# Halving the second batch as well, with smaller loads for the halves and new numbers in the planner's table

## The chip, the cores and the metric

The kernel runs on one core of one Trainium2 chip. The metric is the device time of one execution in microseconds. The kernel before took 1117.67 us, the median of three runs (1117.41 to 1120.12). The profiled execution, from which every duration below is taken, took 1118.3 us, and the span from its first to its last instruction is 1116.5 us.

## What is computed

Two layers, one after the other. The first is attention over 8 batches of 8 heads, 576 positions and 64 numbers per head, in which only scores within `tau` of the row's maximum count. The second is a feed-forward network that mixes each position with the one before it.

```python
# attention, for each batch and head
scores = q @ k.T / 8
thresh = scores.max(-1) - tau
attn = softmax(where(scores >= thresh, scores, -1e9))
x[:, :, head] = attn @ v                      # x: (8, 576, 512)
# feed-forward, on all heads together
x_prev = x shifted by one position
xk = mu_k * x + (1 - mu_k) * x_prev
xr = mu_r * x + (1 - mu_r) * x_prev
k = maximum(xk @ w_k, 0)                      # 512 -> 1024
out = sigmoid(xr @ w_r) * (k * k @ w_v)       # 1024 -> 512
```

## The kernel before

**Attention.** The heads go in four pairs. A *job* is one pair of one batch: `operands` loads `raw` (L408: 128 rows, 64 for each head, with 576 columns of queries, 64 of the last keys and 576 of keys, 1216 columns in all), scales the queries (ACT, L412), rounds everything to `hi` (ACT, L430) and takes the rest `lo` = raw - hi on POOL in two instructions, one for the queries and one for the keys (L436). Eight DMAs within the core's own memory (L455) then stack `hi` and `lo` above each other in `st1` and `st2` for each head, so that a matmul sees both. The first two jobs skip this splitting. `raw` has two buffers, `hi` and `lo` one, `st1` and `st2` three each, of which a job needs two.

A job is worked off in *units*: four units P of 128 queries, each for both heads, and one unit T with the last 64 queries of both heads. A unit counts 2 (P) or 1 (T) on the planner's scale of keys, a whole job 9. For each unit PE makes scores (L517, L506 or L492) in a bank `s`, of which there are two for each half of a unit; DVE takes the maximum (L551), ACT the exponential (L567), DVE masks and sums (L575), POOL normalizes (L600), PE transposes (L624) into one of four banks `w`, and ACT or DVE copies that to `pm` and `pl` (L642, L644). When a group of 256 queries is there, `attend` multiplies it with `v` (L704; two P units, with the T unit's 64 queries in one of the two groups), and DVE copies the result to `xT` and `xE` (L644).

**Feed-forward.** `ffn_chunk` handles 256 positions: POOL and DVE mix (L797, L806), ACT and POOL split (L819, L827), PE multiplies with `w_k` (L849), `w_r` (L891) and `w_v` (L913), DVE makes the product (L919), and the result is stored (L929). There are 18 chunks, two for each batch and two for the last 64 positions of four batches each. A chunk needs a group of 256 queries of all four pairs. The weights come as 20 pieces, each loaded (L338) and brought to two parts by ACT, four DVE instructions (L355, L369, L376, L386), ACT and POOL (L393, L397), with parts of `xT` of the odd batches as scratch.

**Halves.** In batch 0 the four pairs are gone through twice: first with units 0 and 1, then with units 2, T and 3. So the first chunk has its positions after four half jobs. Each half is a job of its own and loads and splits all 1216 columns again, though it uses only its own queries. Batches 1 to 7 are not halved: four jobs of T, 0, 1, 2, 3, after which both their chunks are ready.

**Order.** Nothing is scheduled at run time. Every step is put into a `Plan` with an engine, an assumed duration (`occ`), a key and the buffers it uses; `Plan.order` simulates the engines with these numbers and places, again and again, the step that can start first, with the smaller key at equal times. What it gives is the order of instructions on each engine. PE, ACT, DVE and POOL then run theirs in order, and all loads, shifts and stores stand in one queue, SP's. Feed-forward steps on PE have keys above those of attention (which have 1000 taken off), and so fill PE where attention isn't ready. `LATE` adds 0.3 us to the moment at which attention's steps on PE count as ready, from the planner's time `FROM` on, so that a feed-forward step is put in front where one is there.

Of the kernel before, what the change touches and what calls it, by code (L numbers as in the profile page):

```python
# [8 lines left out]
F32 = mybir.dt.float32  # L9
FR = mybir.dt.float32r  # L10
# [38 lines left out]
class Plan:  # L49
# [3 lines left out]
    HOP, LATE, FROM = 0.05, 0.3, 150.0  # L53
# [58 lines left out]
    def order(self, loose=()):  # L112
# [23 lines left out]
        pipe = 0.0  # L136
# [78 lines left out]
def tile_threshold_attention_then_rwkv_ffn(  # L215
    ctx: ExitStack,
    tc: tile.TileContext,
    qk: bass.AP,
    v: bass.AP,
# [8 lines left out]
    V, A, G, PE, SY = nc.vector, nc.scalar, nc.gpsimd, nc.tensor, nc.sync  # L228

    P = 128
# [10 lines left out]
    KT = S  # L243
    W = 2 * S + ST
# [78 lines left out]
    def weight(j, name, w, c, f, key, wait):  # L323
# [8 lines left out]
        def t():  # L332
# [21 lines left out]
            0.46,  # L354
# [8 lines left out]
        def word(y):  # L363
# [4 lines left out]
            0.46,  # L368
# [6 lines left out]
            0.7,  # L375
# [9 lines left out]
            0.7,  # L385
# [18 lines left out]

    def operands(job, key):
        b, hp = job["b"], job["hp"]
        raw = job["raw"] = sbuf("raw", [P, W], F32, 2)
        add("DMA", DQ, lambda: SY.dma_start(raw.get(), qk[b, hp]), writes=[raw], key=key - PREP - 5, kb=576)  # L408
        add(
            "ACT",  # L410
            0.67,
            lambda: A.activation(raw.get()[:, 0:S], raw.get()[:, 0:S], AF.Copy, scale=small.get()[:, 2:3]),  # L412
            reads=[(small, 2)],
            writes=[raw],
            key=key - PREP,
        )
# [12 lines left out]
        hi, lo = job["hi"], job["lo"] = sbuf("hi", [P, W], FR), sbuf("lo", [P, W], FR)  # L429
        add("ACT", 1.1, lambda: A.activation(hi.get(), raw.get(), AF.Copy), reads=[raw], writes=[hi], key=key - PREP)  # L430
        for y in range(2):
            cs = slice(0, S) if y == 0 else slice(S, W)
            add(
                "POOL",
                1.41 + 0.15 * y,
                lambda cs=cs: G.tensor_tensor(  # L436
                    lo.get()[:, cs], raw.get()[:, cs], hi.get()[:, cs].bitcast(F32), op=ALU.subtract
                ),
                reads=[raw, hi],
                writes=[(lo, y)],  # L440
                key=key - PREP,
            )
        job["st"] = [(sbuf("st1", [P, W], FR, 3), sbuf("st2", [P, S], FR, 3)) for _ in range(2)]
        for h in range(2):
            sl = slice(h * D, (h + 1) * D)
            t1, t2 = job["st"][h]

            up, dn = slice(0, D), slice(D, P)
            for dst, rows, src, n, r in (
                (t1, up, hi, W, (hi, None)),  # L450
                (t2, dn, hi, S, (hi, None)),
                (t1, dn, lo, W, (lo, None)),
                (t2, up, lo, S, (lo, 0)),
            ):
                fn = (lambda dst=dst, rows=rows, src=src, n=n, sl=sl: SY.dma_start(  # L455
                    dst.get()[rows, 0:n].bitcast(F32), src.get()[sl, 0:n].bitcast(F32)
                ))
                add("DMA", DQ, fn, reads=[r], writes=[(dst, rows.start)], key=key - PREP, kb=n // 4)

# [3 lines left out]
    def scores(unit, ss, key):  # L463
        job, c = unit["job"], unit["c"]
        raw = job["raw"]

        def keys(y, z):
            k0 = KT + (ST if unit["kind"] == "P" and y == 0 else 0)
            return slice(k0 + z * HS, k0 + (z + 1) * HS)

        if unit["kind"] == "T" and not job["plain"]:

            hi, lo = job["hi"], job["lo"]
            for v_, src in enumerate((raw, lo)):
                for h in range(2):
# [5 lines left out]
                            bd.get()[sl, v_, sl], src.get()[sl, SM:S].bitcast(F32), AF.Copy  # L481
# [14 lines left out]
        if unit["kind"] == "T" or job["plain"]:  # L496
# [3 lines left out]
            def both():  # L500
                for z in range(2):
                    for h in range(2):
                        hr = slice(h * D, (h + 1) * D)
                        o = ss[1].get()[hr, z, 0:HS] if last else ss[h].get()[:, z, 0:HS]
                        q = slice(SM, S) if last else slice(c * P, (c + 1) * P)
                        PE.matmul(o, raw.get()[hr, q], raw.get()[hr, keys(h, z)], start=True, stop=True)  # L506

            occ = 1.2 if last or key > COLD else 2.3
# [18 lines left out]
    def softmax(unit):  # L527
# [56 lines left out]
        def invert():  # L584
# [5 lines left out]
            0.29,  # L590
# [27 lines left out]
    def transposes(p, y, at, key, to):  # L618
# [9 lines left out]
        occ = 0.109 * len(at)  # L628
# [125 lines left out]
    def ffn_chunk(kind, b0, g, key):  # L754
# [35 lines left out]
        for hc in range(0, NCT, 2):  # L790
# [9 lines left out]
            for j in range(2):  # L800
# [14 lines left out]
                add("DVE", 0.8 if nseg == 1 else 1.57, scale, reads=[diff, mu_sb, *sr], writes=[d], key=key)  # L815
# [122 lines left out]
    halved = {0: ([0, 1], [2, "T", 3])}  # L938
# [3 lines left out]
    for b in range(B):  # L942
        for part, order in enumerate(halved.get(b, (["T", 0, 1, 2, 3],))):
            for hp in range(NPAIR):
                job = dict(ji=len(jobs), b=b, hp=hp, first=n, groups={}, plain=len(jobs) < PLAIN, units=[])
                job.update(tail="T" in order, tg=int(part == 1))
# [89 lines left out]
```

## Time and profile before

| | before |
|---|---|
| median of three runs | 1117.67 us |
| the profiled execution | 1118.3 us, span 1116.5 us |
| PE busy | 1037.2 us (93%) |
| DVE busy | 785.5 us (70%) |
| ACT busy | 736.0 us (66%) |
| POOL busy | 578.6 us (52%) |
| DMA traffic | 117.78 MB, mean 105 GB/s |

The chain of work that ended last runs on PE for 73% of the span, on DVE for 13%, on ACT for 6% and on DMA for 4%. Shares of the whole span hide that the kernel has three stages; the table of windows below shows them apart. In a window's row the figures are its length, then for each engine the busy time with the count of instructions, then the clock granted to PE, the share of the time that the DMA engines were busy, and GB/s. In rows of groups, the last parts are busy time and mean of one, and then the idle time ahead of the group with what ended it. In rows of waits they are the sum, the number of times and the longest one.

### The profile page before, as it was taken

The numbers are of one execution on the slowest core, as the hardware profiler recorded it, in microseconds if no ns is written. First come the engines' busy times: TensorE is split into PE (matmuls) and PEld (weight loads), VectorE is DVE, ScalarE is ACT, GpSimd is POOL, SyncE is SP. The second block draws the span as 40 slices with busy tenths as digits, with TensorE's granted clock in tenths as the row PEclk, the third lists the DMA queues.
The fourth block names the chain that finished last, engine by engine and source line by source line (L and its number), as shares of the span: only waits on it lengthen the run. The fifth ranks groups of instructions, "written<-read, shape, count | busy, mean of one in ns | idle before, by whom it ended". The sixth has DMA issues, their size and how long they took to land.

```text
span 1116.5 us, 19374 instructions
## 1 busy us (share of the span) xinstructions
PE 1037.2 (93%) x6832; PEld 852.4 (76%) x6832; DVE 785.5 (70%) x1712; ACT 736.0 (66%) x1543; POOL 578.6 (52%) x582
## 2 busy tenths in 40 slices
PE   5767878898999999999999999999999989999998
PEld 3446656776877878778789878886788869788887
DVE  6889988877878878877887749765888488422220
ACT  5676776675885876776878666775687557344443
POOL 3575765544564555554656535554465544444441
PEclk8777989999999999999999999999999999999999
DMA  6997365544444435444455314441544141000000
GB/s 218 241 269 226 92 162 132 127 113 119 103 102 119 118 84 139 116 110 111 111 130 137 89 43 121 101 108 37 128 115 118 34 92 39 19 20 20 20 19 19
DMA packets 40639, 117.78 MB, mean 105 GB/s; under 512 B 6752, under 2 KB 6752, under 8 KB 40544
## 3 DMA queue, kind: packets, MB, share of 16 engines
q1 hardware_dynamic: 40544, 116.55, 41.0%
q8 instruction: 55, 0.90, 0.3%
q14 instruction: 40, 0.33, 0.1%
HBM read 44.70 MB, written 9.44 MB: 48 GB/s over the span
## 4 chain that ended last, share of the span: by engine, by line
PE 73%; DVE 13%; ACT 6%; DMA 4%; issue 3%; POOL 1%; SPq 0%; POOLq 0%; ACTq 0%
PE w L913 16%; PE w L849 15%; PE w L704 11%; PE w L624 11%; PE s L517 10%; PE w L891 8%; DVE p L575 4%; PE s L492 2%; ACT p L567 2%; DVE sm L551 2%; DMA raw<-in_qk 1%; DVE sm L585 1%; DMA st<-lo 1%; DMA wk<-in_w_k 1%; DVE mk L806 1%
## 5 line engine op out<-in xcount | busy, mean ns | idle before, releaser
L600 POOL TENSOR_SCALAR p<-p,sm 128x576 f32<-128x576 f32 x288 | 225.5, 792 | 268.9 <-DVE sm L586 227.1
L575 DVE SCALAR_TENSOR_TENSOR p<-s,sm,p 128x576 f32<-128x576 f32 x288 | 232.4, 813 | 58.3 <-ACT p L567 57.1
L551 DVE TENSOR_REDUCE sm<-s 128x1 f32<-128x576 f32 x288 | 210.8, 751 | 40.6 <-PE s L517 27.9
L849 PE MATMUL w<-xk,wk 128*128 128x256 f32 x1728 | 231.0, 284 | 0.0
L913 PE MATMUL w<-wv,k 128*128 128x512 f32 x864 | 221.1, 397 | 0.0
L849 PEld LDWEIGHTS w<-xk,wk 128*128 128x128 f32 x1728 | 216.5, 190 | 1.2 <-issue 0.5
L624 PE MATMUL w<-ident,p 128*128 128x128 f32 x1312 | 197.0, 285 | 19.8 <-POOL p L600 14.8
L567 ACT ACTIVATE p<-s,sm 128x576 f32<-128x576 f32 x288 | 210.2, 730 | 0.6
L624 PEld LDWEIGHTS w<-ident,p 128*128 128x128 f32 x1312 | 156.5, 145 | 58.3 <-POOL p L600 32.1
L913 PEld LDWEIGHTS w<-wv,k 128*128 128x128 f32 x864 | 156.4, 189 | 28.7 <-issue 0.8
L642 ACT ACTIVATE pm<-w 128x512 f32<-128x512 f32 x169 | 99.7, 593 | 98.2 <-PE w L624 96.8
L704 PE MATMUL w<-pm,v 128*64 128x256 f32 (+1 forms) x1024 | 148.4, 425 | 5.2 <-DVE pm L644 4.3
L806 DVE SCALAR_TENSOR_TENSOR mk<-m,mu_sb,xT 128x256 f32<-128x256 f32 x128 | 88.6, 732 | 83.5 <-POOL xk L827 83.4
L517 PE MATMUL s<-st 128*128 128x288 f32 x496 | 119.1, 322 | 27.3 <-DVE p L575 11.7
L827 POOL TENSOR_TENSOR xk<-mk,xk 128x512 fp32r<-128x512 f32 x72 | 94.0, 1306 | 92.8 <-ACT xk L819 87.2
L559 ACT ACTIVATE sm<-sm,small 128x1 f32<-128x1 f32 x288 | 83.5, 290 | 83.4 <-DVE sm L551 80.3
L872 POOL TENSOR_TENSOR k<-r,k 128x512 fp32r<-128x512 f32 x72 | 93.8, 1304 | 81.8 <-ACT k L862 81.5
L704 PEld LDWEIGHTS w<-pm,v 128*64 128x64 f32 x1024 | 71.6, 141 | 64.1 <-issue 10.3
L517 PEld LDWEIGHTS s<-st 128*128 128x128 f32 x496 | 79.7, 193 | 51.4 <-issue 29.0
L436 POOL TENSOR_TENSOR lo<-raw,hi 128x576 fp32r<-128x576 f32 x68 | 102.1, 1518 | 31.2 <-ACT hi L430 23.7
L517 PE MATMUL s<-st,st 128*128 128x288 f32 x496 | 110.6, 305 | 0.0
L891 PE MATMUL w<-wr,xk 128*128 128x512 f32 x432 | 109.4, 396 | 0.4 <-ACT pm L642 0.4
(62 smaller groups left out, 1142.9 us busy)
## 6 DMA issues: line engine op xcount, KB each, us to landing
raw<-in_qk SPq DMA_DIRECT2D x36, 608.0 KB, 5.1
st<-hi SPq DMA_DIRECT2D x68, 304.0 KB, 3.2
st<-lo SPq DMA_DIRECT2D x68, 304.0 KB, 4.3
v<-in_v SPq DMA_DIRECT2D x36, 320.0 KB, 4.2
st<-hi SPq DMA_DIRECT2D x68, 144.0 KB, 3.4
st<-lo SPq DMA_DIRECT2D x68, 144.0 KB, 3.9
out<-sg SPq DMA_DIRECT2D x32, 256.0 KB, 2.0
wk<-in_w_k SPq DMA_DIRECT2D x8, 512.0 KB, 7.5
```

The lines of the kernel that those rows point to most:

```text
L436: lambda cs=cs: G.tensor_tensor(lo.get()[:, cs], raw.get()[:, cs], hi.get()[:, cs].bitcast(F32), op=ALU.subtract),
L517: PE.matmul(ss[y].get()[:, z, 0:HS], l.get()[:, c * P : (c + 1) * P], r.get()[:, keys(y, z)], start=(j == 0), stop=(j == 1),)
L551: lambda sv=sv, col=col: V.tensor_reduce(col(0), sv(), axis=AX.XY, op=ALU.max, negate=True),
L567: lambda sv=sv, pv=pv, col=col: A.activation(pv(), sv(), AF.Exp, bias=col(0)),
L575: lambda sv=sv, pv=pv, col=col: V.scalar_tensor_tensor(pv(), sv(), col(1), pv(), op0=ALU.is_ge, op1=ALU.mult, accum_out=col(2)),
L600: lambda y=y: G.tensor_scalar(p.get()[:, y], p.get()[:, y], sm.get()[:, 3, y : y + 1], 0.0, op0=ALU.mult, op1=ALU.add),
L624: PE.transpose(pt.get()[:, c, :], p.get().rearrange("p y s -> p (y s)")[:, o : o + P], ident.get())
L704: PE.matmul(o.get()[hs, 0:n], vt.get()[:, c, hs], pt[:, 0:n], start=(c == 0), stop=(c == 4))
L806: V.scalar_tensor_tensor(d.get()[:, y, o : o + n], diff.get()[:, y, o : o + n], mu_sb.get()[:, j, hc + y : hc + y + 1], prv[:, hc + y], op ...
L849: PE.matmul(h.get()[:, f], l, r, start=(ct == 0 and i == 0), stop=(ct == NCT - 1 and i == 2))
L891: PE.matmul(z.get(), l, r, start=(ct == 0 and i == 0), stop=(ct == NCT - 1 and i == 2))
L913: PE.matmul(vps.get(), l, r, start=(ft == 0 and i == 0), stop=(ft == NFT - 1 and i == 2))
```

## The change

Batch 1 is now gone through in halves like batch 0 (`HALF = 2`). The jobs of both batches get their own inputs from the host: `qa` has the queries 0 to 255 ahead of the keys (896 columns), `qb` the queries 256 to 575 (960 columns), and all steps of `operands` and `scores` work on these widths. The buffers keep their size. Batch 1 thereby has eight jobs instead of four, and loads its keys and `v` twice. Its last 64 queries go with the second group of 256 and no longer with the first.

The planner's numbers change too: a bank or buffer that comes free also counts 0.3 us later for attention's steps on PE (`hop` in `when`), both delays begin at 200 instead of 150; a DMA is taken to land after 3.5 us at least; some DVE durations are raised, cold matmuls and transposes are taken to be longer; loads may go ahead by a key of 8 instead of 6; and up to key 30 instead of 16 both evictions of a unit go to ACT, and `attend` is cut in five.

```diff
-    HOP, LATE, FROM = 0.05, 0.3, 150.0
+    HOP, LATE, FROM = 0.05, 0.3, 200.0
...
             t = s.ready
+            hop = self.HOP
+            if s.eng == "PE" and s.key < -500 and t > self.FROM:
+                hop += self.LATE
...
-                t = max(t, h[m] + self.HOP)
+                t = max(t, h[m] + hop)
...
-                s.end = max(t + 2.2, pipe + 1.5)
+                s.end = max(t + 3.5, pipe + 2.5)
...
+    HALF = 2
...
-    PREP, PB, VB, COLD, EARLY = 6, 2, 2, 24, 16
+    PREP, PB, VB, COLD, EARLY = 8, 2, 2, 24, 30
...
-        b, hp = job["b"], job["hp"]
-        raw = job["raw"] = sbuf("raw", [P, W], F32, 2)
-        add("DMA", DQ, lambda: SY.dma_start(raw.get(), qk[b, hp]), writes=[raw], key=key - PREP - 5, kb=576)
+        b, hp, nq = job["b"], job["hp"], job["nq"]
+        W = nq + 2 * ST + SM
+        raw = job["raw"] = sbuf("raw", [P, WM], F32, 2)
+        add(
+            "DMA",
+            DQ,
+            lambda: SY.dma_start(raw.get()[:, 0:W], job["src"][b, hp]),
...
-            cs = slice(0, S) if y == 0 else slice(S, W)
+            cs = slice(0, nq) if y == 0 else slice(nq, W)
...
                 (t1, up, hi, W, (hi, None)),
-                (t2, dn, hi, S, (hi, None)),
+                (t2, dn, hi, nq, (hi, None)),
                 (t1, dn, lo, W, (lo, None)),
-                (t2, up, lo, S, (lo, 0)),
+                (t2, up, lo, nq, (lo, 0)),
...
-    halved = {0: ([0, 1], [2, "T", 3])}
+    halved = {j: ([0, 1], [2, "T", 3]) for j in range(HALF)}
...
+                if b < HALF:
+                    job.update(src=(qa, qb)[part], nq=(CH, S - CH)[part], c0=2 * part)
```

Line numbers of the change are higher by 6 to 31 (L408 becomes L419, L455 L477, L517 L541, L624 L648, L704 L728, L849 L873, L913 L937, L929 L953). Three places show what the new table does to the order.

The first is SP's queue in batch 0, the shifts (`st`) of the fourth job (the last pair of the first half) and the load after them. Before:

```order
L455 DMA st_2_314<-hi_302 64x1216
L455 DMA st_2_318<-hi_302 64x576
L455 DMA st_2_318<-lo_316 64x576
L455 DMA st_2_314<-lo_316 64x1216
L455 DMA st_0_349<-hi_302 64x1216
L408 DMA raw_383<-in_qk 128x1216
```

And now, where a load of the next half stands between the fourth job's shifts:

```order
L477 DMA st_2_267<-hi_264 64x896
L419 DMA raw_281<-in_qb 128x960
L477 DMA st_2_283<-hi_264 64x256
L477 DMA st_2_283<-lo_277 64x256
L477 DMA st_2_267<-lo_277 64x896
L419 DMA raw_310<-in_qb 128x960
```

The transfers are the same in number, each is shorter, and the next loads stand further ahead in the queue.

The second is PE's order where the first chunk ends (its last products with `w_v`) and batch 1 begins. Before, these are the rows behind the chunk's last step; scores (L517) and transposes (L624) follow, and the next feed-forward step comes 25 rows behind that last one:

```order
L913 MATMUL w_1258<-wv_0_1572,k_0_1036 128x512 x3
L517 MATMUL s_1626<-st_1_1440 128x288 x2
L517 MATMUL s_1626<-st_1_1440,st_1_1449 128x288 x2
L517 MATMUL s_1634<-st_0_1380 128x288 x2
L517 MATMUL s_1634<-st_0_1380,st_0_1387 128x288 x2
L624 MATMUL w_1646<-ident,p_1563 128x128 x4
L624 MATMUL w_1653<-ident,p_1563 128x128 x4
L624 MATMUL w_1661<-ident,p_1563 128x128
```

Now, from a few rows behind the ninth `attend` on:

```order
L937 MATMUL w_1595<-wv_0_1242,k_0_966 128x512 x3
L648 MATMUL w_1737<-ident,p_1624 128x128 x4
L648 MATMUL w_1744<-ident,p_1624 128x128
L541 MATMUL s_1747<-st_2_1667 128x288 x2
L541 MATMUL s_1747<-st_2_1667,st_2_1677 128x288 x2
L937 MATMUL w_1595<-wv_0_1407,k_0_966 128x512 x3
L648 MATMUL w_1766<-ident,p_1696 128x128 x4
L937 MATMUL w_1595<-wv_0_1602,k_0_966 128x512 x3
```

The first chunk's last steps are spread among the scores of batch 1; the last of them has moved from before the ninth `attend` to behind the tenth.

The third is SP's queue in batch 1, at the shifts of the first job of its second half. Before, both stores of the first chunk stood together, between a load and the second head's shifts of batch 1's second job:

```order
L408 DMA raw_1576<-in_qk 128x1216
L421 DMA v_1584<-in_v 128x640
L929 DMA out<-sg_1116 128x512 x2
L455 DMA st_0_1698<-hi_1520 64x1216
L455 DMA st_0_1705<-hi_1520 64x576
```

Now the first store stands among the first head's shifts:

```order
L477 DMA st_2_1847<-hi_1841 64x960
L953 DMA out<-sg_1413 128x512
L436 DMA v_1872<-in_v 128x640
L477 DMA st_2_1885<-hi_1841 64x320
L477 DMA st_2_1885<-lo_1855 64x320
L477 DMA st_2_1847<-lo_1855 64x960
```

Three shifts and a load of `v` have moved behind a store that waits for DVE's product of the first chunk.

More of the change, by code (lines that the diff above doesn't have):

```diff
@@ L218, in tile_threshold_attention_then_rwkv_ffn @@
     qk: bass.AP,
+    qa: bass.AP,
+    qb: bass.AP,
     v: bass.AP,
@@ L374, in weight @@
             "DVE",
-            0.7,
+            0.85,
             lambda: V.scalar_tensor_tensor(
@@ L428, in operands @@
             return
-        hi, lo = job["hi"], job["lo"] = sbuf("hi", [P, W], FR), sbuf("lo", [P, W], FR)
-        add("ACT", 1.1, lambda: A.activation(hi.get(), raw.get(), AF.Copy), reads=[raw], writes=[hi], key=key - PREP)
+        hi, lo = job["hi"], job["lo"] = sbuf("hi", [P, WM], FR), sbuf("lo", [P, WM], FR)
+        add(
+            "ACT",
+            0.04 + 0.88e-3 * W,
+            lambda: A.activation(hi.get()[:, 0:W], raw.get()[:, 0:W], AF.Copy),
+            reads=[raw],
+            writes=[hi],
+            key=key - PREP,
+        )
         for y in range(2):
-            cs = slice(0, S) if y == 0 else slice(S, W)
+            cs = slice(0, nq) if y == 0 else slice(nq, W)
             add(
                 "POOL",
-                1.41 + 0.15 * y,
+                2.45e-3 * (cs.stop - cs.start),
                 lambda cs=cs: G.tensor_tensor(
@@ L442, in operands @@
             )
-        job["st"] = [(sbuf("st1", [P, W], FR, 3), sbuf("st2", [P, S], FR, 3)) for _ in range(2)]
+        job["st"] = [(sbuf("st1", [P, WM], FR, 3), sbuf("st2", [P, S], FR, 3)) for _ in range(2)]
         for h in range(2):
@@ L464, in scores @@
         job, c = unit["job"], unit["c"]
-        raw = job["raw"]
+        raw, nq = job["raw"], job["nq"]
+        if unit["kind"] == "P":
+            c -= job["c0"]
         def keys(y, z):
-            k0 = KT + (ST if unit["kind"] == "P" and y == 0 else 0)
+            k0 = nq + (ST if unit["kind"] == "P" and y == 0 else 0)
             return slice(k0 + z * HS, k0 + (z + 1) * HS)
@@ L504, in both @@
                         o = ss[1].get()[hr, z, 0:HS] if last else ss[h].get()[:, z, 0:HS]
-                        q = slice(SM, S) if last else slice(c * P, (c + 1) * P)
+                        q = slice(nq - ST, nq) if last else slice(c * P, (c + 1) * P)
                         PE.matmul(o, raw.get()[hr, q], raw.get()[hr, keys(h, z)], start=True, stop=True)
-            occ = 1.2 if last or key > COLD else 2.3
+            occ = 1.2 if last or key > COLD else 3.0
             add("PE", occ, both, reads=[raw], writes=list(ss.values()), key=key - 1000, lat=occ + 0.25)
@@ L589, in softmax @@
             "DVE",
-            0.29,
+            0.33,
             invert,
@@ L813, in scale @@
                             )
-                add("DVE", 0.8 if nseg == 1 else 1.57, scale, reads=[diff, mu_sb, *sr], writes=[d], key=key)
+                add("DVE", 0.9 if nseg == 1 else 1.6, scale, reads=[diff, mu_sb, *sr], writes=[d], key=key)
                 add(
@@ L945, in tile_threshold_attention_then_rwkv_ffn @@
                 job = dict(ji=len(jobs), b=b, hp=hp, first=n, groups={}, plain=len(jobs) < PLAIN, units=[])
-                job.update(tail="T" in order, tg=int(part == 1))
+                job.update(tail="T" in order, tg=int(part == 1), src=qk, nq=S, c0=0)
+                if b < HALF:
+                    job.update(src=(qa, qb)[part], nq=(CH, S - CH)[part], c0=2 * part)
                 for u in order:
@@ L1001 @@
     np_, m = h // 2, 512
-    qk = np.concatenate([q, k[:, :, m:], k], axis=2).transpose(0, 1, 3, 2).reshape(b, np_, 2 * d, -1)
+    qk, qa, qb = (
+        np.concatenate([part, k[:, :, m:], k], axis=2).transpose(0, 1, 3, 2).reshape(b, np_, 2 * d, -1)
+        for part in (q, q[:, :, :256], q[:, :, 256:])
+    )
     vp = np.zeros((b, np_, 128, 5, 2, d), v.dtype)
@@ L1017 @@
         qk=qk,
+        qa=qa,
+        qb=qb,
         v=vp.reshape(b, np_, 128, -1),
```

21 lines of the change are left out of this document (12 added, 9 removed).

## The prediction

> **What bounds the kernel now.** I read the 40 slices first, then a table of windows cut where the slices change, then the waits of each stage. The slices (tenths of busy time, 28 us each; PEclk is the clock granted to PE):
>
> ```profile
> PE   5767878898999999999999999999999989999998
> DVE  6889988877878878877887749765888488422220
> PEclk8777989999999999999999999999999999999999
> DMA  6997365544444435444455314441544141000000
> ```
>
> PE is full from the tenth slice or so on; ahead of that DVE is fuller than PE, with DMA at its fullest in slices 2 and 3 and a low clock. The windows:
>
> ```profile
> 0.00:28.00 28.00, 14.58 (x52) 9.24 (x53) 17.08 (x33) 15.23 (x29) 9.40 (x14) 0.88 0.66 218
> 28.00:168.00 140.00, 107.71 (x599) 80.21 (x595) 126.33 (x238) 99.96 (x208) 93.05 (x79) 0.84 0.74 198
> 168.00:280.00 112.00, 101.00 (x679) 80.08 (x675) 90.09 (x195) 74.04 (x168) 54.93 (x60) 0.97 0.49 122
> 280.00:973.00 693.00, 675.04 (x4670) 558.54 (x4669) 524.30 (x1183) 489.95 (x1050) 366.99 (x383) 1.00 0.40 97
> 973.00:1117.00 144.00, 138.91 (x843) 124.35 (x842) 27.75 (x66) 56.86 (x91) 54.27 (x49) 1.00 0.06 21
> ```
>
> The cuts are the end of batch 0's attention (168), of batch 1's (280) and of all attention (973). Up to 168 **DVE** bounds: 126.3 of 140 us, while PE idles for 13.4 + 32.3 us. Later **PE** bounds, with 11.0 us idle up to 280 and 18.0 up to 973. Behind that stand only chunks, which the chain of waits shows back to back; the last one:
>
> ```profile
> 1084.27 11.30 PE w L849 x96
> 1095.58 5.46 PE w L891 x24
> 1101.03 10.89 PE w L913 x48
> ```
>
> A chunk is 27.65 us of PE. The change alters neither the scores, transposes and products on PE nor their number, and in both orders some 5.2 chunks remain behind the last `attend` (feed-forward steps ahead of it, times these durations: 349.9 us before, 348.6 now). So the time moves only by what PE idles or runs slowly before 973, and most of that lies before 280.
>
> **The terms, one by one.** The sum is made against the profiled execution's 1118.3 us (span 1116.5, and 1.8 around it); it lies 0.6 above the median of 1117.67.
>
> *First load.* The chain's first pieces:
>
> ```profile
> 1.18 4.34 DMA raw<-in_qk
> 6.88 1.44 ACT L412 ACTIVATE raw<-raw,small 128x576 f32<-128x576 f32 x2
> ```
>
> The load falls from 608 to 448 KB; a scaling, 0.72 us, handles 256 columns instead of 576, which is 0.4 less. The load's saving lies between 0 (a fixed cost) and 4.34 x 160/608 = 1.1. I take 0.6, in all **-1.0**, all on the path.
>
> *Shorter transfers in batch 0.* A split job loads 608 KB and shifts 2 x (2 x 304 + 2 x 144) = 1792 KB. With 896 columns this is 448 and 1152, with 960 it is 480 and 1280. Over eight loads and six splits batch 0 saves 1152 + 3328 = 4480 KB. What DMA does from 28 to 112, and the largest pieces of the chain there:
>
> ```profile
> DMA packets 6390, 20.62 MB, mean 245 GB/s; under 512 B 951, under 2 KB 951, under 8 KB 6382
> q1 hardware_dynamic: 6382, 20.53, 87.8%
> 33.62 11.65 DMA wk<-in_w_k
> 45.28 6.38 DMA st<-lo
> ```
>
> At 245 GB/s it is 18.7 us of transfer, in a stage where DMA was busy 88% and 18 us of the chain are transfers. But DVE did weights meanwhile. What it waited there in all, of 13.7 us idle:
>
> ```profile
> DVE sm L551 <- PE s L517: 5.3, 8, 1.7
> DVE p L575 <- ACT p L567: 2.1, 4, 0.9
> ```
>
> Only the wait for scores can come from late operands; 0 to 5.3, and I take 60%, **-3**.
>
> A rule of the skill speaks against this. The median times from issue to landing:
>
> ```profile
> raw<-in_qk SPq DMA_DIRECT2D x36, 608.0 KB, 5.1
> st<-hi SPq DMA_DIRECT2D x68, 304.0 KB, 3.2
> st<-hi SPq DMA_DIRECT2D x68, 144.0 KB, 3.4
> ```
>
> The Trainium skill, "DMA: Bandwidth & Descriptors", section "Anatomy of one DMA", gives each transfer a fixed cost of about 2.0 us, plus bytes at 436 GB/s. By that, cutting 144 KB to 64 would save some 0.2 us (an estimate from that page), and batch 1's 40 more transfers would each pay 2 us again. The two shift rows agree that size hardly matters where the queue is free; by it this term would be near 0 and the sum -4. I keep the bytes, for the stage in question is the one where the DMA engines are full.
>
> *Less on POOL and DVE in batch 0.*
>
> ```profile
> L436 POOL TENSOR_TENSOR lo<-raw,hi 128x640 fp32r<-128x640 f32 x34 | 53.9, 1586 | 0.0
> L436 POOL TENSOR_TENSOR lo<-raw,hi 128x576 fp32r<-128x576 f32 x34 | 49.3, 1450 | 31.2 <-ACT hi L430 23.7 <-ACT p L567 4.7 <-issue 2.0
> L644 DVE COPY pm<-w 128x512 f32<-128x512 f32 x119 | 81.6, 686 | 28.3 <-PE w L624 27.7
> L642 ACT ACTIVATE pm<-w 128x512 f32<-128x512 f32 x169 | 99.7, 593 | 98.2 <-PE w L624 96.8
> ```
>
> A split is 3.04 us of POOL for 1216 columns, so 2.24 for 896 and 2.40 for 960: six splits save 4.1. POOL isn't the bound, but DVE slows beside it. One place shows it, the rows of DVE, POOL and PE:
>
> ```profile
> 214.44 3.44 DVE L806 SCALAR_TENSOR_TENSOR mk<-m,mu_sb,xT 128x256 f32<-128x256 f32 x2
> 214.50 3.09 POOL L436 TENSOR_TENSOR lo<-raw,hi 128x576 fp32r<-128x576 f32 x2
> 218.72 0.68 PE L517 MATMUL s<-st 128*128 128x288 f32 x2 [2.34 <-issue]
> L806 DVE SCALAR_TENSOR_TENSOR mk<-m,mu_sb,xT x128: 463/481/1768, 58.7 to 1052.3; 128x256 f32<-128x256 f32 x128
> ```
>
> Two mixes of 0.48 us (the median; the row has minimum, median, maximum in ns) took 3.44 beside a split, and PE idled 2.34 until the scores could start. So of POOL's 4.1 between none and all comes back to DVE; I take **-2**. The larger `EARLY` takes five copies of 0.686 off DVE (the order has 119 before, 114 now); ACT gets them at 0.593 and had 40 us idle between 28 and 168. That is -3.4 of DVE, of which I take **-2.5**, since conversions of weights wait behind.
>
> *Later filling.* Ahead of batch 0's last `attend`, the order now has 20.8 us of chunk on PE instead of 26.3, and a little more of attention. As DVE bounds that stage, PE owes up to 5.5 us later, from 0 where the idle time after it takes them; I take two thirds, **+3.8**. (By batch 1's last `attend` the order has caught up: 57.8 against 55.3.)
>
> *Batch 1.* The gap between the first and the second chunk (25 rows of PE without a chunk's step) is filled. That stretch, and the largest wait at batch 1's end:
>
> ```profile
> 168.00:182.00 14.00, 11.14 (x71) 7.84 (x69) 13.03 (x31) 9.06 (x21) 5.86 (x9) 1.00 0.53 160
> PE w L704 <- DVE pm L644: 2.9, 1, 2.9
> ```
>
> PE idles 2.9 us in each, 0 to 5.8 to gain. I take **-3**. Against it stand four more jobs: 40 more issues on SP, 4 x (320 + 320 + 640) = 5120 KB (loads, `v`, shifts), which lift 122 GB/s to 169 over 112 us, under what the engines gave before; and POOL's 4 x (2.24 + 2.40 - 3.04) = 6.4 us. If they press on DVE as at 214, 0 to 6.4; I take **+2**, nearer the lower end, since only this one idle time of PE ahead of scores stands above 2 us among eight splits of that stage. At a job's start the chain of loading, scaling, rounding, splitting and shifting must fit into a half job (112/8 = 14 us). By the rows it is at most 5.1 + 0.8 + 1.2 + 2.4 + 4.3 = 13.8 (the three rows below, and those above), partly ahead of time through two buffers. So 0, with up to 1 us for each of four new boundaries.
>
> ```profile
> L412 ACT ACTIVATE raw<-raw,small 128x576 f32<-128x576 f32 x36 | 27.8, 776 | 6.9 <-DMA raw<-in_qk 6.8
> L430 ACT ACTIVATE hi<-raw 128x1216 fp32r<-128x1216 f32 x34 | 41.5, 1220 | 17.1 <-PE s L492 15.5 <-DMA st<-lo 1.2 <-ACT pl L642 0.5
> st<-lo SPq DMA_DIRECT2D x68, 304.0 KB, 4.3
> ```
>
> *Slack on banks.* Of what PE waits between 280 and 973, these two kinds end with a bank that comes free:
>
> ```profile
> PE s L517 <- DVE p L575: 3.4, 7, 0.9
> PE w L624 <- DVE xE L644: 1.7, 4, 0.5
> ```
>
> That is 5.1 us in eleven waits, and a chunk's step put in front (three products, 3 x 0.118) covers 0.35 of each, some 3.9. I take **-1.5**, from 0 to -5, since the step must be there.
>
> **Sum**: -1.0 - 3 - 2 - 2.5 + 3.8 - 3 + 2 - 1.5 = -7.2, so 1111.1; I forecast **1111**, which is 6.7 below the median. Its own range is 1105 to 1114.
>
> **Rivals.**
> 1. *Nothing to be measured.* DVE ends batch 0 no earlier, because its work is the same (conversions of 20 pieces, 38 half units), and PE still pays the 3.8 us. With first load, -1.5 for banks and half of batch 1's filling, -1.0 - 1.5 - 1.5 + 3.8 is 0: about 1117.5. For it speaks DVE's 90% in that stage. Against it, DVE's 13.7 idle us and the smaller copies.
> 2. *Slower.* Each new job's split meets DVE instructions as at 214 to 218 and holds PE up for 2.34 us. Four jobs, two splits each: at all eight it is 18.7 us, at four 9.4. With the gains that don't depend on it (-1.0 - 2.5 + 3.8 - 1.5 = -1.2) and four meetings, 1118.3 + 8.2 = 1126. From two meetings on (4.7 - 1.2 = 3.5) it is a loss that can be measured. For it: half of batch 1's splits stand where `mk` rows run. Against it: the new splits are shorter, and batch 0 had six of them in a stage that hid them.
> 3. *A gain twice as large.* The new order puts chunks earlier: 99.7 us of them ahead of batch 2's end instead of 87.9, 188.8 instead of 167.7 ahead of batch 4's. DVE is then less pressed per batch, and PE, idle 18.0 us between 280 and 973, could lose half of that more: 1111 - 7 = 1104.
>
> PE's clock speaks for 1 too. The granted clock from 28 to 168 is 0.84, and a first pair of scores that took 0.50 us in full clock took 0.82 after an idle time of 4.45:
>
> ```profile
> 101.24 0.82 PE L492 MATMUL s<-hi,bd 128*128 128x288 f32 x2 [4.45 <-DVE p L575]
> 130.86 0.50 PE L492 MATMUL s<-hi,bd 128*128 128x288 f32 x2 [1.06 <-DVE p L575]
> ```
>
> With 5.5 us less of chunk in batch 0, PE has more such gaps; 0.3 us more on perhaps ten of the 38 half units is 3 us, which ends in rival 1.
>
> **How the numbers follow.** Forecast 0.52, rival 1 0.22, rival 2 0.17, rival 3 0.09. A measurement here tells 0.3%, 3.4 us, from no change. Faster: 0.52 + 0.09 = 0.61; the same: 0.22; slower: 0.17. The range runs from rival 3, 1104, less 1, to rival 2 with three meetings, 1118.3 + 7.0 - 1.2 = 1124, less the 2 that shorter splits save: 1103 to 1122.
>
> **What would show it.** The window up to batch 0's last copy to `xT` (168.3 before) should end at 163 to 166, with DVE's waits for scores under 3 us and DMA under 80% from 28 to 112. PE's idle time in batch 1 should be 8 us or less, with no wait over 2 us on scores. If batch 0 ends at 168 or later, the first terms are wrong; if PE idles over 13 us in batch 1 and `mk` rows beside `lo` exceed 1.5 us, rival 2 holds. PE's idle time from batch 2 on near 10 us would show rival 3.

## The result and the profile after

The changed kernel takes 1089.16 us (median of four runs, 1088.13 to 1090.30) against 1118.89 for the kernel before on the same chip: a ratio of 0.9737, 95% interval [0.9719, 0.9755], so 29.7 us faster, where 6.7 were forecast. The sign was right; the time lies 14 us below the range, and 15 below the rival with the largest gain. The profiled execution took 1088.13 us with a span of 1086.3, that is 30.2 less than before.

The slices of the page after (27 us each):

```profile
PE   4666899999999999999999999999999999999998
DVE  6999999779887788777877877766878498222220
PEclk8888999999999999999999999999999999999999
DMA  6784467556445344453544434541545041000000
```

PE is full from the sixth slice on, where it was full from about the tenth. DVE fills slices 2 to 7 without a dent, and DMA's peak in slices 2 and 3 is down from 9 tenths to 7 and 8. The windows of after, with the cuts of before (the last one 30 us earlier, as the span is 30 us shorter):

```profile
0.00:28.00 28.00, 12.88 (x43) 8.00 (x44) 18.54 (x37) 13.75 (x28) 9.77 (x14) 0.87 0.65 218
28.00:168.00 140.00, 106.38 (x656) 77.50 (x655) 133.38 (x255) 104.06 (x226) 96.01 (x87) 0.92 0.62 178
168.00:280.00 112.00, 108.56 (x768) 89.50 (x765) 94.23 (x207) 86.33 (x194) 66.06 (x70) 1.00 0.61 161
280.00:943.00 663.00, 652.91 (x4534) 543.73 (x4533) 503.54 (x1147) 475.37 (x1022) 355.44 (x371) 1.00 0.41 100
```

The counts in brackets are the quickest way to compare, since both kernels run the same 6832 matmuls. By 280 us PE has done 43 + 656 + 768 = 1467 of them; before it was 1330. At the mean of 149 ns for each (PE's 1019.4 us by 6832), the 137 more are some 20 us, so more than half of the gain is made by then. (The kinds of matmul differ in length; the measure below, which takes them apart, gives 17 of 30.9 us up to batch 1's end.) From 28 to 168 DVE does 133.4 us of work instead of 126.3, and PE's granted clock is 0.92 instead of 0.84.

Cut where batch 0's and batch 1's last copies to `xT` and the last of all stand, the windows of before are

```profile
0.00:168.34 168.34, 122.63 (x649) 89.57 (x650) 143.40 (x270) 115.19 (x236) 102.79 (x92) 0.85 0.73 201
168.34:277.11 108.77, 97.77 (x651) 77.07 (x652) 88.06 (x192) 72.30 (x162) 54.39 (x58) 0.97 0.49 122
277.11:963.98 686.87, 668.91 (x4653) 553.96 (x4654) 522.78 (x1178) 490.43 (x1052) 362.18 (x379) 1.00 0.40 98
```

and of after

```profile
0.00:158.85 158.85, 111.03 (x646) 79.51 (x646) 142.84 (x270) 112.54 (x240) 97.92 (x93) 0.90 0.62 184
158.85:263.60 104.75, 100.39 (x686) 80.85 (x687) 88.62 (x196) 78.89 (x178) 65.02 (x67) 1.00 0.66 171
263.60:931.77 668.17, 658.08 (x4615) 549.05 (x4614) 514.46 (x1172) 485.67 (x1045) 360.26 (x378) 1.00 0.41 102
```

Batch 0 ends 9.5 us earlier with nearly the same count of matmuls (646 for 649) and no less idle time on PE (47.8 us for 45.7): PE's busy time shrinks by 11.6. Busy time times clock is 104.2 before and 99.9 now, so by this estimate some 4 of that is work that was moved (chunk steps), and the rest goes with the clock. Batch 1 ends after 4.0 us less with 35 more matmuls, idle 4.4 us instead of 11.0. The other six batches take 18.7 us less with 38 fewer.

The stages hold different shares of the chunks, so a measure is wanted that takes these out. I call **lag** the start of the n-th `attend`'s copy to `xT`, less the time that PE's steps ahead of it in its order take undisturbed (chunks by the three rows of the last chunk in the prediction; transposes 0.109, scores 0.132, `attend`'s products 0.231 and 0.284 us each). It holds everything that PE idles or runs slowly. Prices that both kernels pay alike drop out of the differences, and only these are used. At attends 8, 16 and 64 (the ends of batch 0, 1 and 7) it is 75.2, 96.4 and 138.8 before, and 69.5, 79.4 and 107.9 after. So of 30.9 us, 5.7 are gained in batch 0, 11.3 in batch 1 and 13.9 behind it.

DVE's waits from 28 to 168 in after (line waiting and what ended it, sum, times, longest), where scores had cost 5.3 us in 8 waits:

```profile
DVE p L599 <- ACT p L591: 2.1, 5, 1.0
...
DVE sm L575 <- PE s L541: 0.8, 2, 0.6
```

DMA from 28 to 112 in after, 87.8% and 20.53 MB before:

```profile
q1 hardware_dynamic: 6269, 17.10, 67.8%
```

And PE's waits from 280 to 943 in after, where waits on banks (`p L575`, `xE L644`) had been 5.1 us in eleven and "issue" 6.1:

```profile
PE w L648 <- POOL p L624: 3.4, 6, 1.0
PE s L541 <- DVE p L599: 2.3, 5, 0.7
PE w L728 <- DVE pm L668: 1.9, 1, 1.9
...
PE s L541 <- issue: 0.8, 1, 0.8
```

### The profile page after: what moved, and what is told of

The parts are those of the page before. It is cut to its first block, busy times and chain, and to the rows that moved or that the text cites. A ratio compares the mean times of both kernels' runs of the same rounds, so it can differ in the third digit from the quotient of the medians.

```text
span 1086.3 us, 19493 instructions
## 1 busy us (share of the span) xinstructions
PE 1019.4 (94%) x6832; PEld 842.7 (78%) x6832; DVE 777.1 (72%) x1707; ACT 736.4 (68%) x1556; POOL 581.6 (54%) x590
## 4 chain that ended last, share of the span: by engine, by line
PE 74%; DVE 15%; ACT 4%; DMA 2%; issue 2%; SPq 1%; POOL 1%; POOLq 0%; ACTq 0%; DVEq 0%
PE w L873 17%; PE w L937 15%; PE w L728 12%; PE s L541 10%; PE w L648 10%; PE w L915 8%; DVE p L599 4%; DVE sm L575 3%; DVE mk L830 2%; PE s L516 2%; ACT p L591 1%; DVE sm L609 1%; DVE xT L392 1%; DVE xT L382 1%; DMA st<-lo 1%
## 5 line engine op out<-in xcount | busy, mean ns | idle before, releaser
L624 POOL TENSOR_SCALAR p<-p,sm 128x576 f32<-128x576 f32 x288 | 226.8, 798 | 222.8 <-DVE sm L610 160.3
L599 DVE SCALAR_TENSOR_TENSOR p<-s,sm,p 128x576 f32<-128x576 f32 x288 | 232.2, 813 | 59.4 <-ACT p L591 55.9
L873 PE MATMUL w<-xk,wk 128*128 128x256 f32 x1728 | 233.8, 284 | 0.0
L575 DVE TENSOR_REDUCE sm<-s 128x1 f32<-128x576 f32 x288 | 210.8, 749 | 31.5 <-PE s L541 21.3
L937 PE MATMUL w<-wv,k 128*128 128x512 f32 x864 | 220.9, 396 | 0.9 <-ACT pm L666 0.9
L648 PE MATMUL w<-ident,p 128*128 128x128 f32 x1312 | 197.0, 282 | 24.9 <-POOL p L624 23.6
L873 PEld LDWEIGHTS w<-xk,wk 128*128 128x128 f32 x1728 | 217.6, 189 | 1.7 <-issue 0.5
L648 PEld LDWEIGHTS w<-ident,p 128*128 128x128 f32 x1312 | 154.0, 144 | 67.1 <-POOL p L624 44.2
L937 PEld LDWEIGHTS w<-wv,k 128*128 128x128 f32 x864 | 155.5, 188 | 28.7 <-ACT pm L666 1.4
L666 ACT ACTIVATE pm<-w 128x512 f32<-128x512 f32 x174 | 102.5, 591 | 69.9 <-PE w L648 69.0
L728 PE MATMUL w<-pm,v 128*64 128x256 f32 (+1 forms) x1024 | 142.7, 414 | 2.4 <-DVE pm L668 1.9
L830 DVE SCALAR_TENSOR_TENSOR mk<-m,mu_sb,xT 128x256 f32<-128x256 f32 x128 | 84.1, 697 | 73.0 <-POOL xk L851 73.0
L541 PE MATMUL s<-st 128*128 128x288 f32 x496 | 116.5, 316 | 17.6 <-issue 8.7
L458 POOL TENSOR_TENSOR lo<-raw,hi 128x576 fp32r<-128x576 f32 (+2 forms) x76 | 106.8, 1422 | 39.9 <-ACT hi L448 38.9
L728 PEld LDWEIGHTS w<-pm,v 128*64 128x64 f32 x1024 | 69.6, 137 | 55.7 <-issue 8.6
L541 PE MATMUL s<-st,st 128*128 128x288 f32 x496 | 109.0, 301 | 0.0
L541 PEld LDWEIGHTS s<-st 128*128 128x128 f32 x496 | 79.6, 191 | 37.6 <-issue 20.4
```

The costliest lines, as they stand in the source:

```text
L458: lambda cs=cs: G.tensor_tensor(lo.get()[:, cs], raw.get()[:, cs], hi.get()[:, cs].bitcast(F32), op=ALU.subtract),
L541: PE.matmul(ss[y].get()[:, z, 0:HS], l.get()[:, c * P : (c + 1) * P], r.get()[:, keys(y, z)], start=(j == 0), stop=(j == 1),)
L575: lambda sv=sv, col=col: V.tensor_reduce(col(0), sv(), axis=AX.XY, op=ALU.max, negate=True),
L599: lambda sv=sv, pv=pv, col=col: V.scalar_tensor_tensor(pv(), sv(), col(1), pv(), op0=ALU.is_ge, op1=ALU.mult, accum_out=col(2)),
L624: lambda y=y: G.tensor_scalar(p.get()[:, y], p.get()[:, y], sm.get()[:, 3, y : y + 1], 0.0, op0=ALU.mult, op1=ALU.add),
L648: PE.transpose(pt.get()[:, c, :], p.get().rearrange("p y s -> p (y s)")[:, o : o + P], ident.get())
```

## The experiments

Each ratio compares runs on one chip. The kernel before had medians of 1117.4 to 1119.2 us on the chips used, so times from different chips are compared to within 2 us.

### Code or numbers?

`p_only` is the kernel before with the planner's numbers alone; `s_only` has the halves and the smaller loads alone. From the change they are

```diff
# p_only
-    HALF = 2
+    HALF = 1
...
-                if b < HALF:
-                    job.update(src=(qa, qb)[part], nq=(CH, S - CH)[part], c0=2 * part)
# s_only: the durations of before, FROM = 150, and
-                hop += self.LATE
+                hop += 0.0
...
-    PREP, PB, VB, COLD, EARLY = 8, 2, 2, 24, 30
+    PREP, PB, VB, COLD, EARLY = 6, 2, 2, 24, 16
```

> The kernel before with the change's planner numbers alone (durations, slack on banks from 200 on, loads further ahead, EARLY 30): batch 1 isn't halved and batch 0's halves load all 1216 columns. Theory N (the numbers of the planner give most of the 30 us): 1096 or less. Theory H (the halves of batch 1 and the smaller loads give most, since 11 of the 31 us came in batch 1 and 6 in batch 0): 1104 or more, with batch 0 ending near 168 us as before and PE idle near 11 us up to batch 1's end. If the parts add up, this run's gain and that of the run with the halves alone make 30 us together.

> The kernel before with the halves of both batches and their smaller loads alone; all planner numbers as before. Theory H: 1105 or less, most of the gain inside the first 280 us. Theory N: 1112 or more: batch 0 ends earlier, at 160 us or so, and the gain is lost again, since the order has only 42 us of chunks ahead of batch 1's end instead of 58, and PE idles for what is missing.

`p_only` took 1102.26 us, ratio 0.9860 [0.9830, 0.9891]; `s_only` 1132.11, ratio 1.0127 [1.0095, 1.0160]. (`p_only` keeps batch 0's halves, at full width.) Numbers alone bring 15 us, code alone costs 15, both together bring 30. They are not two terms of a sum. `p_only` lies between what its two theories had said.

### How much an order varies for no reason

The order is made by a greedy planner, so any number may move it. `s_null` and `b_null2` are the kernel before with some assumed durations moved by 0.01 us or less (`s_null` also counts a load as 608 KB instead of 576), and `a_null1` and `a_null2` the change with such moves (`a_null1` also counts a load as 5% smaller). For `s_null` the numbers are written out; its code has `nq` (576) and `W` (1216) in their place:

```diff
# s_null, in the kernel before
-    kb=576
+    kb=608
-            0.67,
+            0.06 + 1.05e-3 * 576,
-            1.1,
+            0.04 + 0.88e-3 * 1216,
-                1.41 + 0.15 * y,
+                2.45e-3 * (cs.stop - cs.start),
# a_null1
-            kb=W // 2,
+            kb=W * 9 // 19,
-            0.06 + 1.05e-3 * nq,
+            0.07 + 1.05e-3 * nq,
-            0.04 + 0.88e-3 * W,
+            0.05 + 0.88e-3 * W,
# a_null2; b_null2 likewise in the kernel before
-    EV = ("ACT", 0.49), ("DVE", 0.6)
+    EV = ("ACT", 0.5), ("DVE", 0.61)
-                0.186,
+                0.19,
-                0.715,
+                0.72,
```

> The kernel before with its assumed durations rounded otherwise, by 0.01 us or less, and a load counted at 608 KB instead of 576; nothing else. The order comes out a little different. If orders that differ for no reason scatter little, 1117 plus or minus 3; if single orders scatter as much as the parts of the change seem to bring (6 to 15 us), it may lie anywhere from 1105 to 1130, and the differences of single runs above say little.

> The change with two assumed durations of ACT raised by 0.01 us and loads counted 5% smaller; nothing else. As 0.01 us made the kernel before 7 us faster, this and the next run tell how much of the change's 29 us is its single order. If it is the parts: 1086 to 1093. If the change's order is a lucky one among its like: 1095 to 1105.

> The change with four other assumed durations raised by 0.004 to 0.01 us (evictions, threshold, normalization). Parts: 1086 to 1093. A lucky order: 1095 to 1105.

> The kernel before with the same four assumed durations raised by 0.004 to 0.01 us. If the kernel before had an unlucky order: 1107 to 1113, as the first such run (1111). If orders scatter evenly about 1117: anywhere from 1110 to 1125.

`s_null` took 1111.23 (0.9929 [0.9904, 0.9955]), `b_null2` 1111.36 (0.9935 [0.9913, 0.9958]), `a_null1` 1086.67 (0.9716 [0.9700, 0.9732]), `a_null2` 1096.09 (0.9803 [0.9789, 0.9818]). With the two kernels themselves there are three orders of each kind: 1119, 1111, 1111 and 1089, 1087, 1096. A single order thus stands some 5 us to either side of its kind for no reason that one would change a kernel for, while the kinds differ by 23 (means 1113.8 and 1090.6). `p_only` and `s_only` have the code of `s_null`; against the mean of its kind, 1113.8, numbers alone bring 12 us and code alone costs 18, each in a single order. A part that is worth under about 8 us can't be read from one order, and for the large parts I undid them in a second order too, that of `a_null1`.

### Parts undone, one at a time

The runs with `a_` and `olddma` start from the change, those with `n1_` from `a_null1`.

```diff
# a_half1, n1_half1
-    HALF = 2
+    HALF = 1
# a_nobank, n1_nobank
-                hop += self.LATE
+                hop += 0.0
# a_oldprep
-    PREP, PB, VB, COLD, EARLY = 8, 2, 2, 24, 30
+    PREP, PB, VB, COLD, EARLY = 6, 2, 2, 24, 16
# a_wide, n1_wide: 1216 columns for every half
-                if b < HALF:
-                    job.update(src=(qa, qb)[part], nq=(CH, S - CH)[part], c0=2 * part)
# a_olddur, n1_olddur: the durations of before; olddma: the landing alone
-                s.end = max(t + 3.5, pipe + 2.5)
+                s.end = max(t + 2.2, pipe + 1.5)
```

> The change with batch 1 whole again; batch 0's halves keep their smaller loads and the planner its new numbers. My forecast had the halves of batch 1 at -3 + 2 = -1 us, which would make this 1090. Theory H in its narrow form (the halves of batch 1 give the 11 us that batch 1 got faster): 1098 to 1101, with PE idle near 11 us between batch 0's and batch 1's end.

> The second order of the change, with batch 1 whole. Theory (halves of batch 1 bring some 6 us, chunks reach PE earlier in batch 1): 1092 to 1098, with the lag at attend 16 higher by 4 or more than in the second order (76.7). Rival (that difference lies within the scatter of orders): 1082 to 1090, or over 1102.

> The change without the slack on banks (a bank that comes free counts 0.05 us later again, the delay of ready steps stays from 200 on). My forecast had the slack at -1.5 us: 1090.5. Theory K (the slack on banks gives most of the 14 us that lie behind batch 1): 1098 to 1104, with PE idle near 18 us between 280 us and the end of attention instead of 10, and its waits for banks back at 5 us or more.

> The second order of the change (1086.7 us), without the slack on banks. Theory (the slack on banks spares PE waits and slow groups all through the kernel once PE has chunks at hand): 1098 to 1106, as in the first order (1104.5), with the lag behind batch 1 growing by 40 us or more between attends 16 and 64 where it grows by 32 in the second order. Rival (the 15 us were scatter of single orders): 1082 to 1094.

> The change with loads only 6 ahead and EARLY at 16, as before; all else as in the change. I had put the five copies that EARLY takes off DVE at -2.5 us: 1092. Rival theory E (loads further ahead are what the shorter jobs of batch 1 need): 1098 or more, with DVE or PE waiting for shifts in batch 1.

> The change with the durations of before in the planner (DMA landing, DVE, cold PE), all else as in the change. Theory D (with halves of batch 1 and without these durations batch 1 goes wrong, which is why the halves alone cost 15 us): 1100 or more, and batch 1 loses at least 8 us to the change. Rival (the slack and the prefetch mend it): 1093 or less.

> The second order of the change, with the old durations in the planner for the landing of a DMA, DVE's steps and cold PE. Theory (the order must be made with durations near the true ones, or shifts and banks come later than planned): 1105 to 1116, with the lag at attend 16 at 85 or more (76.7 in the second order). Rival (scatter): 1082 to 1094.

> The change with the old landing of a DMA alone (2.2 us at least instead of 3.5, other durations as in the change). Theory (shifts and loads planned to land too early are what costs): 1105 to 1115, that is most of the 24 us of all old durations. Rival (DVE's and cold PE's durations matter): 1086 to 1097.

> The change, but all half jobs load, split and shift the full 1216 columns, so batch 1 moves 4 x 2720 KB more than before and batch 0 as much as before. My terms for the smaller transfers and splits in batch 0 were -1 - 3 - 2 = -6, and a run with batch 1 whole showed 7 us between full and smaller loads. If the width matters in both batches: 1100 or more, with DMA nearly full from 28 to 168 us and PE waiting on scores at starts of jobs. If DMA is hidden: 1093 or less.

> The second order of the change, with the halves loading, splitting and shifting all 1216 columns. Theory (the smaller loads are what lets halves pay, about as much as in the first order): 1105 to 1118, with the DMA share from 28 to 100 at 0.85 or more and the lag at attend 24 at 100 or more (81.8 in the second order). Rival (the 26 us were one bad order): 1084 to 1098.

| undone | in the change | ratio to before | in `a_null1`'s order | ratio to before | dearer by |
|---|---|---|---|---|---|
| (nothing) | 1089.16 | 0.9737 [0.9719, 0.9755] | 1086.67 | 0.9716 [0.9700, 0.9732] | |
| smaller loads and splits | 1114.97 | 0.9969 [0.9954, 0.9984] | 1116.98 | 0.9993 [0.9970, 1.0016] | 26, 30 |
| durations | 1113.32 | 0.9954 [0.9939, 0.9968] | 1115.88 | 0.9966 [0.9948, 0.9984] | 24, 29 |
| landing of a DMA alone | 1107.88 | 0.9907 [0.9893, 0.9922] | | | 19 |
| slack on banks | 1104.46 | 0.9869 [0.9837, 0.9900] | 1092.03 | 0.9765 [0.9749, 0.9781] | 15, 5 |
| halves of batch 1 | 1095.19 | 0.9788 [0.9762, 0.9813] | 1096.34 | 0.9804 [0.9789, 0.9819] | 6, 10 |
| `PREP`, `EARLY` | 1096.46 | 0.9796 [0.9770, 0.9823] | | | 7 |

The parts of the first column add up to 78 us (26, 24, 15, 6, 7), 2.6 times the gain: the large ones don't bring their share without the others. Widths and durations stand above the scatter in both orders. The slack and the halves have the same sign twice, the size of the slack is open between 5 and 15, and `PREP` with `EARLY` is not told apart from scatter. Batch 1 whole (`a_half1`) and `PREP` with `EARLY` undone (`a_oldprep`) both came out between what their two theories had named.

**Widths.** With `p_only` and `a_half1` there is a square: batch 1 whole, full widths 1102.3, small 1095.2; batch 1 halved, full widths 1115.0, small 1089.2. Halving batch 1 costs 12.7 us with full widths and brings 6.0 with small ones. What the widths do to the stage stands in two windows of `a_wide`,

```profile
28.00:60.00 32.00, 19.53 (x99) 13.30 (x96) 28.72 (x56) 21.37 (x45) 21.98 (x20) 0.76 0.96 237
160.00:220.00 60.00, 50.82 (x349) 43.96 (x348) 41.29 (x93) 39.77 (x84) 36.77 (x36) 0.91 0.85 219
```

and the same two of after:

```profile
28.00:60.00 32.00, 20.87 (x106) 13.75 (x105) 31.25 (x56) 21.46 (x47) 21.97 (x19) 0.77 0.73 213
160.00:220.00 60.00, 56.39 (x414) 45.78 (x412) 50.52 (x111) 43.32 (x101) 37.11 (x41) 1.00 0.65 168
```

With full widths DMA is busy 96% and 85%, DVE and PE are less full in both, and in batch 1 PE's clock falls to 0.91. PE's waits for `st`, 1.2 us in after from 28 to 280, are 8.1 in `a_wide` (its waits for a bank that DVE frees, `p L599`, grow as much, from 8.9 to 16.5):

```profile
PE s L541 <- DMA st<-lo: 8.1, 4, 3.9
```

The rule of the Trainium skill that I had weighed ("DMA: Bandwidth & Descriptors", "Anatomy of one DMA") gives a transfer a fixed cost and makes the bytes of a small one nearly free. That section describes transfers that GpSimd issues; the ones here stand in SP's queue. After and `a_wide` issue the same transfers and differ in their columns, in DMA and in the scaling, rounding and splitting behind it, and in the order that the planner makes from these. 26 and 30 us between them in two orders, with the DMA share as shown, speak against taking the bytes as free where the queue is full. No run narrows the DMAs alone, so how much of the 26 to 30 us is bytes and how much is work on ACT and POOL stays open.

A second loss follows from the order. Chunk steps ahead of batch 1's end, counted in PE's order, are 57.8 us in after and 81.6 in `a_wide`, of the three chunks (83 us) that can be ready by then. So `a_wide` begins batch 2 with nothing left to fill PE with; its lag grows there from 92.8 to 109.5, in after from 79.4 to 82.1. PE in `a_wide`:

```profile
300.00:410.00 110.00, 101.56 (x697) 81.78 (x694) 87.53 (x201) 75.41 (x170) 54.96 (x60) 0.97 0.47 119
```

**Durations.** The lag of `olddma` at attends 8, 16, 24 and 64 is 71.0, 88.1, 100.6 and 128.3, of after 69.5, 79.4, 82.1 and 107.9. 17 of the 20 us arise in batches 1 and 2. Their rows, in `olddma`,

```profile
158.00:280.00 122.00, 111.33 (x762) 89.59 (x761) 90.12 (x202) 86.80 (x194) 68.01 (x71) 1.00 0.58 153
274.40:398.00 123.60, 118.14 (x792) 95.50 (x793) 94.02 (x201) 85.89 (x186) 63.68 (x65) 1.00 0.43 107
```

in after,

```profile
158.00:280.00 122.00, 117.62 (x822) 95.84 (x821) 104.06 (x228) 92.46 (x209) 74.78 (x80) 1.00 0.62 163
263.60:366.80 103.20, 103.20 (x747) 86.85 (x746) 82.91 (x191) 80.71 (x178) 58.25 (x62) 1.00 0.48 120
```

and, for batch 1, in `n1_olddur`

```profile
158.00:280.00 122.00, 106.76 (x690) 85.76 (x687) 94.07 (x211) 82.64 (x187) 67.66 (x70) 0.93 0.59 155
```

and `s_only`, the dearest of all:

```profile
158.00:280.00 122.00, 104.90 (x676) 82.52 (x677) 91.39 (x212) 79.71 (x184) 67.18 (x71) 0.90 0.56 149
```

In the same 122 us PE does 822 matmuls in after (849 in `a_null1`, 801 in `a_null2`), 762, 690 and 676 in the others, and in batch 2 it idles not at all in after and 5.5 us in `olddma`. What ends its waits in `olddma`'s batch 1 are seven things of 0.8 to 2.3 us and two smaller ones, the largest

```profile
PE s L541 <- DMA st<-lo: 2.3, 2, 1.2
PE s L541 <- DVE p L599: 1.7, 3, 0.9
```

So late operands are part of it (0 us in after there), but no single wait carries the 19 us. The shifts of this stage, in `olddma` (count, size, median us from issue to landing), lie above the 2.2 us that its order was made with:

```profile
st<-hi SPq DMA_DIRECT2D x3, 144.0 KB, 4.1
...
st<-hi SPq DMA_DIRECT2D x4, 64.0 KB, 2.5
```

That the order made with the short landing loses is shown, as the 19 us stand above the scatter (at attend 24 `olddma`'s lag is 100.6, that of `a_null2`, the dearest order like the change's, 91.3). How the loss spreads over so many small waits and slow groups is not.

**Slack.** From 280 to 930 PE does in after

```profile
280.00:930.00 650.00, 639.91 (x4469) 533.44 (x4469) 499.76 (x1138) 471.20 (x1018) 350.23 (x366) 1.00 0.42 102
```

and in `a_nobank`

```profile
280.00:930.00 650.00, 632.39 (x4355) 523.04 (x4353) 491.03 (x1109) 456.92 (x989) 336.64 (x354) 0.99 0.41 102
```

that is 7.5 us more idle and 114 matmuls fewer. In the second order it is 640.07 us and 4458 with the slack, 638.72 and 4455 without, so the harm isn't always done. PE's idle time from 280 to 960 is 18.0 us in `a_nobank`, as its theory had said. But the waits of attention's steps on banks, on which alone the slack acts, came back only in part: 2.3 us in after, 3.7 in `a_nobank` (`p L599`, `xE L668`, `r L881`). More grew at chunk steps, which wait for a bank (`pm L666`, 0.9 us in after) or for operands (`xk`, 0 in after):

```profile
PE w L937 <- ACT pm L666: 2.8, 4, 1.6
PE w L873 <- ACT xk L843: 2.5, 1, 2.5
...
PE w L873 <- POOL xk L851: 1.5, 2, 1.0
```

So what the slack is worth is seen in its sign, but by which path it works is not.

### Parts alone in the kernel before

```diff
# b_bank, in the kernel before, from 150
+            hop = self.HOP
+            if s.eng == "PE" and s.key < -500 and t > self.FROM:
+                hop += self.LATE
...
-                t = max(t, h[m] + self.HOP)
+                t = max(t, h[m] + hop)
# b_dur, in the kernel before (with the other durations)
-                s.end = max(t + 2.2, pipe + 1.5)
+                s.end = max(t + 3.5, pipe + 2.5)
```

> The kernel before with the slack on banks alone, from 150 on like its other delay. Theory K (the slack keeps short waits off PE wherever chunks can be put in front, with either structure): 1101 to 1106, as taking it out of the change cost 15 us. Rival (the slack is worth that only with the change's other numbers, since what counts is how well the order as a whole fits): 1113 or more.

> The kernel before with the new durations alone (landing of a DMA, DVE's steps, cold PE). Theory (the durations alone bring what the new numbers bring in the kernel before, 15 us): 1100 to 1107, with the lag at attend 16 at 92 or less (96.4 before). Rival (they matter only with the halves, whose half jobs leave less time for loads and shifts): 1109 to 1121, the scatter of orders like before's.

`b_bank` took 1117.56 (0.9987 [0.9970, 1.0003]), `b_dur` 1112.60 (0.9965 [0.9949, 0.9981]). Neither differs from the three orders of before by more than these do among themselves. The 24 to 29 us that the durations are worth in the change they do not bring alone in the kernel before, as the rival said. Whether it is the halves, the narrow loads or the other numbers that they need, no run tells: `p_only`, which has all numbers and no halves in batch 1, took 1102.26.

`a_null1`, at 1086.67, is the fastest kernel of the study; that it beats the change by 2.5 us is within the scatter of orders, and no reason to prefer its numbers.

## Why the prediction was right and wrong

**Right: the bound, and batch 0's sum.** The bound was DVE up to 168, and part of the loss lay in late operands beside a full DMA queue. Three of the signs asked for came: DVE's waits for scores under 3 us (0.8), DMA under 80% (67.8), PE's idle time in batch 1 under 8 us (3.4). The terms of batch 0 make -8.5 + 3.8 = -4.7; its lag fell by 5.7. Its end came at 158.85, earlier than the 163 to 166 that I named, and close to what the terms ahead of the +3.8 make of 168.3 (159.8). Term by term this is partly luck. The first scores start 0.5 us earlier (7.22 for 7.71), not 1.0. DVE's waits for scores fell by 4.5, not 3. Of the five copies four, 2.7 us, left DVE by batch 0's end, near the 2.5. The -2 for less POOL work did not come: the conversions and mixes took some 2 us less, but a small step of `sm` became dearer, before and after:

```profile
L585 DVE TENSOR_SCALAR sm<-sm 128x2 f32<-128x2 f32 x16 | 4.8, 301 | 0.5
L609 DVE TENSOR_SCALAR sm<-sm 128x2 f32<-128x2 f32 x17 | 8.6, 509 | 0.4
```

**Wrong: batch 1, "-3" and "+2".** The lag that it adds fell by 11.3, not 1. I looked at one gap of 14 us and one long wait, instead of the stage: PE idled 11.0 us there, ran at 0.97, and added 21.2 us of lag. The +2 for POOL's extra splits did not come. A meeting as at 214 did:

```profile
245.37 3.35 DVE L830 SCALAR_TENSOR_TENSOR mk<-m,mu_sb,xT 128x256 f32<-128x256 f32 x2
245.33 3.10 POOL L458 TENSOR_TENSOR lo<-raw,hi 128x576 fp32r<-128x576 f32 x2 [0.26 <-ACT hi L448]
```

But PE had an `attend` to do meanwhile and then idled 0.31 us, and 3.4 us from 168 to 280 in all. (That the 2.34 us at 214 came from the meeting was a guess: the row has "issue", which names no cause.) Halving, undone alone, is 6 to 10 us, of which scatter is a part.

**Wrong: the slack "-1.5", and what lies behind batch 1.** I counted waits of PE on banks and covered them with steps. The lag added behind batch 1 fell by 13.9. Undone, the slack is 5 to 15 us; the sign was right, the size was not, and that it works by sparing attention's waits on banks is shown for 1.4 us only (3.7 less 2.3). Rival 3 named an idle time "near 10" from batch 2 on, and 10.1 is what it is. It was priced at 7 us since I let it act on PE's idle time alone.

**The failed step** is the one ahead of the terms: "the time moves only by what PE idles or runs slowly before 973". That holds, but the terms were then taken from waits, gaps and DVE's work, and PE's slow running was put at nothing. PE's idle time fell by 12.4 us (79.3 to 66.9 over the span), its busy time for the same matmuls by 17.8 (1037.2 to 1019.4). Some 12 of the 17.8 go with the clock, by an estimate from the windows: busy time times what the clock lacks to 1 adds up to 22.0 us before and 10.2 after. For this there was no term, only a doubt in the other direction ("PE's clock speaks for 1 too"); where the other 6 come from stays open. The planner's durations, the second largest part of the change, had no term either: I read the orders that they gave and costed instructions that move, as if an order's fit to the true durations were worth nothing. Undone, they cost 24 and 29 us. (A small slip beside these: the chunks behind the last `attend` are 5.3 by the sums given, 18 x 27.65 less 349.9, and not 5.2; nothing hangs on it.)

**The rivals.** Nothing and slower are refuted for the change as a whole, though slower is what the halves do by themselves (`s_only`), and not by mixes that meet splits: the three pairs of `mk` in its batch 1 took 1.28, 0.87 and 0.87 us. Evened chunks hold as a description: chunk steps on PE between the batch ends are 37, 42, 43, 46, 44, 61 and 55 us after, 29, 33, 37, 42, 66, 57 and 59 before. They are not enough as a cause, since `olddma` has 44, 51, 37, 49, 45 and 48 up to batch 6 and is 19 us slower.

## What to carry to other kernels

When a change moves most of a static order, the bounding engine's idle time is not all that can be won: its slow groups count too, so compare busy times at equal work, and the work done by a given time. A planner's assumed latencies are part of the kernel, and a change of structure is judged together with latencies like those of the trace. Before a few microseconds are believed, make two or three orders that differ for no reason; here they spread over 8 to 9 us.

## What the hardware showed that I had not expected

The clock granted to PE in batch 0 rose although PE idled no less. From 60 to 80 us PE was busy for more of the time before than after, and yet its clock was lower. Before:

```profile
60.00:80.00 20.00, 14.69 (x81) 11.14 (x77) 16.82 (x37) 12.49 (x29) 13.75 (x14) 0.74 0.98 304
```

After:

```profile
60.00:80.00 20.00, 13.18 (x87) 8.34 (x86) 18.85 (x39) 16.07 (x35) 11.14 (x12) 0.96 0.92 318
```

There 87 matmuls, of a somewhat other mix, took less time than 81 (a transpose 319 ns in the mean instead of 365, the first product of a score 324 instead of 427). The Trainium skill, "TensorE: Matmul & The Clock Gate", "Part 1: The HAM clock gate", ties the clock to how busy PE has lately been. The rows of whole stages agree (0.84 where PE idles a quarter of the time, 1.00 where it idles 3%). These two seem not to, but a low clock itself lengthens the busy time: times the clock, PE did 10.9 us of work in before's row and 12.7 in after's. So by the work done they don't speak against it, and what came first, more work at hand or the higher clock, no run here tells.
